# Delta-rule attention and a GELU layer on one core: another order of all engines' work

## The chip, the cores and the metric

The kernel runs on one core of one Trainium2 chip. The core has five engines that each work through a queue of their own: TensorE (PE in the profile; PEld is its weight load), VectorE (DVE), ScalarE (ACT), GpSimd (POOL) and SyncE (SP, which here issues DMAs only). ACT and POOL can issue DMAs too. The metric is the device time of one execution in microseconds (us), as the median of several runs; lower is better.

## The reference

Four batches of eight heads run a delta rule over 768 steps with a state of 48 x 48 per head; the outputs of all heads are put side by side, 3072 rows of 384, and go through two matrix products with a tanh GELU between them.

```python
k_n = k / (norm(k) + 1e-6)
for t in range(S):                       # S = 768, state is (4, 8, 48, 48)
    y[:, :, t] = q[:, :, t] @ state
    v_old = state @ k_n[:, :, t]
    state = state + beta[:, :, t] * outer(k_n[:, :, t], v[:, :, t] - v_old)
x = y.transpose(0, 2, 1, 3).reshape(3072, 384)
out = gelu_tanh(x @ w_in) @ w_out        # w_in 384 x 2048, w_out 2048 x 384
```

## The kernel before

The 768 steps are cut into 12 chunks of 64. A chunk is worked in two units of 16 heads, so 24 units, numbered 0 to 23; unit u belongs to chunk u // 2. Nothing in the kernel is a loop on the chip: every step is a word of its own, and each word is one or several instructions on one engine.

**A unit** (`prep`, L470 to L618). The words kc, kb and qb (L484 to L488) copy k, scaled k and q into bf16 with heads side by side. A transpose follows, on PE (T, Tk, Tc, Tb, Tq, L494, evicted by kT words) or by a DMA from SP (turn, L512). The words GM, GQ, G2 and G (L530) are products of keys with keys and queries, in quarters of the array; ln, wpm, wpq and wp (L534) write them under a triangular mask on DVE. Then the inverse of a 64 x 64 triangle for each head is made in five rounds. X10 and X11 (L564 on POOL, L566 on DVE) make the first guess. In round i, Ai (PE, eight products, L575), rti (DVE, 2I plus the product, L587) and Bi (PE, eight products) follow one another, and the result is copied from PSUM into the two diagonal blocks of `bd`. That copy has three forms, and the planner picked one for each round of each unit: two half copies bdei0 and bdei1 on ACT or DVE; one half bdfi0 and one whole with a scale, bdfi1 (L338); or one whole copy xii followed by two SBUF copies bdci0 and bdci1 on POOL or DVE (L617).

**A chunk** (`chain`, L620 to L714). K (L647) and Q are products of the state with keys and queries, vs (L657) scales v, R (L660) adds it to K's result, U (L670) multiplies by the inverse, Un copies that, S (L682) and Sn (L689) bring the state forward, O (L695) adds to Q's result, On copies it, and X on PE with xT, or a DMA turnx, transposes it for the layer. **The layer** (`mlp`, L716 on) has 16 up words per chunk (three matmuls each, L724), four gelu words (ACT, L728), eight down words (four matmuls each, L735: down0i and down1i for the two halves of the rows), two copies Z0 and Z1, and stores out.

**Around them.** The word norms sq, sum, pow, eps, nsq or nsa, inv and ib (L454 to L467) work out the norms of k; pow is ACT's square root in the first three chunks and POOL's power after these. The words k, q and v load one chunk's part, beta the betas, w1 and w2 (L441, L443) the weights in two halves each. tri, pad, bdz, ident, mup, mlo, two, half and the like set up constants. fill0 to fill69 (L394) are matmuls of zeros with zeros, of which a plan uses as many as it likes; nothing reads them.

**The order.** `ORDER` (L17 to L111) is a text of 1,708 words, found by a planner outside the kernel. A word is a step's name; a letter after a colon names its engine where the step may run on several (p, a, d, g, s for PE, ACT, DVE, POOL and SP; without it the first engine allowed is taken), a number after @ the PSUM bank where its result goes. `Flow.order` puts the words into one queue per engine in the order of the text, and `Flow.emit` works out the semaphore waits that the data need. Which copy, engine, bank and place in the queue a step gets is thus set by the text alone, and each engine runs its queue strictly in order.

```python
for i, word in enumerate(text.split()):
    word, _, bank = word.partition("@")
    name, _, e = word.partition(":")
    o = self.by[name]
    o.on, o.at = ENGINES[e] if e else o.engs[0], i
    ...
    self.queue.append(o)
    self.queues[o.on].append(o)
```

Of the kernel before, what the change touches and what calls it, by code (L numbers as in the profile page):

```python
# [16 lines left out]
ORDER = """  # L17
beta01:a one pad1 k0x1.11:a k0x0.01:a bdz0:g upone1 wz:d fill23@0 fill20@1 fill46@0 fill16@1 fill63@4 fill26@1 half:d fill25@0 fill12@2
fill54@5 ident pad3:g k0x0.10 tmplz:d tmpl0 k0x1.00:a k0x1.10:a k0x1.01:a mmup:d pad0 mmlo:d mlo0 fill64@0 k0x0.00 mlo1 tmpl1 two:d triln1:d
triwpm3:d triwpm1:d ladj16:d fill37@1 identf k0x0.11 ident2 ladj32:d fill28@4 sq.0a:d fill65@3 mup0 k1.00 fill56@4 sum.0a triln0:d fill41@1  # L20
fill52@6 beta00 betaT0@3 betaN000 betaN001 betaN010 betaN011 k1.01 epsb k1.10:a fill45@2 beta11:a k1.11 fill22@1 beta10 sq.0b:g tabS pow.0a
eps.0a twob:d J1.1@3 sum.0b q0.1 mup1 nsa.0a v0.11 inv.0a ib.0a upone0 v0.10 pow.0b fill55@2 q0.0:a eps.0b nsa.0b sq.1:d fill36@0 kb.0 kc.1
bdz1:g k2.10 fill49@2 inv.0b ib.0b:g kb.1:g betaT1@0 kc.0 Tc.1@1 fill9@2 betaA111 betaA110 betaA101 sum.1 pow.1 eps.1:g nsq.1:g kTc.1 q1.1
fill60@4 Tb.0@2 kTb.0 Tc.0@4 kTc.0 Tb.1@1 inv.1 triwpm0:d betaA100 ib.1 GM.0@6 ln.0 kb.3:g v1.11:a v0.01 X11.0 wpm.0 kTb.1:a GM.1@4 ln.1
X10.0 v0.00:a qb.0:a Tq.0@1 wpm.1 kc.3 Tk.3@2 triln3 A1.0@0 X10.1:d kTq.0 GQ.0@4 k2.00:a kTk.3:a q1.0:a X11.1 C1.1 rj1.1 rt1.0 B1.0@0 k2.01
pad2 kb.2 wpq.0 bde10.0 kc.2:d GM.3@6 ln.3 B1.1@1 bde10.1:d bde11.0 A2.0@0 rt2.0 bde11.1 A2.1@1 rt2.1 Tk.2@3 triwpm2 B2.0@2 B2.1@0 qb.1:a
v1.00 Tq.1@1 v1.10 v1.01 wpm.3 bde21.0:d k2.11 sq.2 sum.2 bde20.0 A3.0@2 fill1@4 fill4@5 fill42@4 fill14@5 q2.0 bdf20.1 bdf21.1:d A3.1@0
rt3.0 B3.0@2 kTk.2:a GM.2@4 rt3.1 triln2 ln.2 w2.1 qb.2:a bdz4:g bdz3:g X10.3 kTq.1:a X11.3 w1.1 A1.3@0 pad5:g pow.2 B3.1@1 k3.10 GQ.1@6
wpm.2 rt1.3 kc.5 k4.10 q2.1 bdf30.0 bdf31.0 A4.0@2 rt4.0 vs.1 B1.3@0 R0b.0:g bdf30.1 bdf31.1 A4.1@1 bdz2:g wpq.1 v2.00 bdf10.3 qb.3:g
eps.2:g B4.0@2 bde41.0 nsq.2:g bde40.0 X11.2 rt4.1 q3.0 X10.2 A1.2@4 rt1.2 B4.1@1 bde41.1:d w1.0 bde40.1 Tq.2@3 kTq.2 B1.2@4 bde10.2  # L30
triwpm4:g A5.0@5 rt5.0 A5.1@1 rt5.1 bde11.2 bdf11.3:d k3.01 B5.0@2 bde50.0 A2.2@3 rt2.2 B5.1@4 bde50.1:d bde51.0 k3.00 bde51.1 B2.2@0
bde21.2 bde20.2 inv.2 A2.3@1 rt2.3 R0a.0:g U.0@4 Un.0:d B2.3@1 A3.2@0 rt3.2 q4.0 Tq.3@2 O.0@4 On.0:d fill6@3 bde21.3 qb.5:g B3.2@0 bde20.3
A3.3@1 rt3.3 kTq.3:a GQ.3@6 X.0@2 xT.0:d B3.3@1 triwpm5:g bdf30.2 bdf31.2 A4.2@0 rt4.2 bdf30.3 bdf31.3:d up4.0@2 up12.0@4 up13.0 k3.11 wpq.3
ib.2:g kb.5:g B4.2@0 up5.0 up6.0 up7.0 up14.0 A4.3@1 up15.0 up0.0@6 q3.1 tabG bde41.2:d bde40.2 up1.0 up2.0 A5.2@0 rt4.3 gelu1.0 pad4:g
kb.4:g kc.7 up3.0 B4.3@1 w2.0 kc.4:g sq.3:g sum.3 k4.00 k5.10 q4.1 gelu3.0 gelu0.0 qb.4:g T.4@2 kT.4:a T.5@4 rt5.2 bde41.3:d bde40.3:d kT.5
pow.3 eps.3:g up8.0@6 up9.0 v2.11 A5.3@0 rt5.3 k5.00:a G2.5@2 ln.5 bdz5:g kc.6:g X11.5 k4.01:a G2.4@4 S.0@0 Sn.0 ln.4 X11.4 X10.4 G.4@2 wp.4
up10.0 qb.9:a up11.0 gelu2.0 nsq.3:g qb.6:g qb.7:g k4.11 K.1@0 R.1 inv.3 ib.3:g kb.6:g kb.7:g v3.11 G.5@4 wp.5 B5.2@2 sq.4 down10.0@3 A1.4@1
down00.0@0 bde51.2 rt1.4 kc.8 down01.0 X10.5 sum.4 pow.4 eps.4:g B5.3@4 bdf50.3 B1.4@1 bde10.4 k5.01 bde11.4:d down11.0 A1.5@5 rt1.5
down02.0 k5.11 sq.5:g kc.10:g A2.4@1 v4.10 v4.11 rt2.4 turn.7 v2.10 bdf51.3 bde50.2 B1.5@4 bde10.5:d bde11.5 down03.0 Z0.0 B2.4@2 v3.10
bde21.4:d kc.9:g U.1@6 Un.1 A2.5@5 rt2.5 q5.0 down12.0 GQ.2@0 wpq.2 Q.1@6 bde20.4 A3.4@2 turn.6 v3.00:a rt3.4 G2.7@4 O.1 On.1 S.1@0 Sn.1  # L40
nsq.4:g down13.0 inv.4 ib.4:g X.1@2 B2.5@6 xT.1:d kb.9:g v4.01 sum.5 pow.5 eps.5:g kb.8:g Z1.0 bde20.5 B3.4@7 bdf30.4 turn.9 fill47@3 v3.01
ln.7 bdf31.4 v2.01:a up0.1@0 up1.1 up2.1 up3.1 bde21.5:d gelu0.1 q6.1 A4.4@2 rt4.4 qb.8:a up8.1@4 up9.1 k7.00 A3.5@3 rt3.5 B4.4@2 bde41.4
k7.11 G2.6@0 ln.6 G.7@6 wp.7 q7.0 up10.1 B3.5@3 bde31.5 bde30.5 X10.6 up11.1 gelu2.1 up4.1@0 up5.1 up6.1 G.6@6 bde40.4:d A4.5@3 k6.10:a
# [755 lines left out]
```

## Time and profile before

| | |
|---|---|
| median of 3 runs | 263.77 us (263.1 to 265.27) |
| span of the profiled execution, first to last instruction | 258.8 us |
| DVE busy in the span | 209.5 us, 358 instructions |
| ACT busy | 185.1 us, 295 instructions |
| POOL busy | 136.2 us, 198 instructions |
| bytes read and written in HBM | 20.64 and 4.72 MB |

The profile is of one execution. The times of the three runs have more around them than the span: the median is 5.0 us above it. A row such as "L587 DVE TENSOR_TENSOR rt<-ps,two 128x512 bf16<-128x512 f32 x71 | 47.6, 683 | 5.4 <-PE ps L575 4.9" reads: line, engine, operation, what is written from what, shapes, number of instructions, us busy in all, mean ns of one, us that the engine was idle just before them, and what ended most of that. The windows give for each stretch the us that each engine was busy and, in brackets, its instructions; then the TensorE clock that was granted as a share of full speed, the busy share of the DMA engines, and the rate of the DMAs.

### The profile page before, as it was taken

To read this page: it belongs to the slowest core of one execution; us is meant where nothing else is said; L and a number is where in the kernel's file an instruction comes from. 1 tells how busy PE (TensorE), PEld (TensorE's weight loads), DVE (VectorE), ACT (ScalarE), POOL (GpSimd) and SP (SyncE) were. 2 spreads that over 40 slices of the span, in tenths; PEclk is the share of its full clock that TensorE was granted. 3 is DMA by queue.
4 is the path that set the end of the run, shared out by engine and by line. 5 is a ranking of instruction groups with operands and counts; after the bars stand their busy time and mean duration, and the time that the engine had idled before them with its cause. 6 is when DMAs were issued, how large, how long until landed. Compare 5 with 4: busy or idle time off the path is not lost.

```text
span 258.8 us, 12244 instructions
## 1 busy us (share of the span) xinstructions
PE 242.1 (94%) x5490; PEld 189.6 (73%) x5490; DVE 209.5 (81%) x358; ACT 185.1 (72%) x295; POOL 136.2 (53%) x198
## 2 busy tenths in 40 slices
PE   7769789998999999999999999989989999999994
PEld 2446669666867878778877787768868878877672
DVE  6898998988999798899999788997778879895000
ACT  0679899667786878687978879866948745754452
POOL 4469767997558978688158255643654204130000
PEclk9985999999999999999999999999999999999999
DMA  5999999879999877959729959536935720004122
GB/s 88 200 191 182 212 185 200 135 132 151 164 198 146 167 107 134 159 102 165 160 47 157 155 96 185 53 74 123 155 66 106 128 48 4 3 5 124 30 63 61
DMA packets 116788, 31.46 MB, mean 122 GB/s; under 512 B 110848, under 2 KB 115968, under 8 KB 116736
## 3 DMA queue, kind: packets, MB, share of 16 engines
q1 hardware_dynamic: 98096, 24.24, 57.4%
q0 software_dynamic: 2880, 3.15, 7.5%
q10 hardware_dynamic: 15760, 3.30, 7.4%
q8 instruction: 43, 0.70, 1.1%
q14 instruction: 9, 0.07, 0.1%
HBM read 20.64 MB, written 4.72 MB: 98 GB/s over the span
## 4 chain that ended last, share of the span: by engine, by line
PE 81%; DVE 8%; POOL 4%; issue 3%; ACTq 2%; ACT 1%; POOLq 0%
PE ps L724 24%; PE ps L735 24%; PE ps L575 20%; PE ps L530 4%; PE ps L647 3%; PE ps L670 2%; PE ps L695 2%; ACTq L432 2%; DVE rt L587 1%; PE ps L682 1%; DVE wp L534 1%; POOL nrm L458 1%; DVE ln L534 1%; PE ps L394 1%; POOL bd L564 1%
## 5 line engine op out<-in xcount | busy, mean ns | idle before, releaser
L332 ACT ACTIVATE bd<-ps 64x512 bf16<-64x512 f32 x127 | 72.8, 587 | 20.5 <-PE ps L575 18.7
L724 PE MATMUL ps<-xT,W 128*128 128x256 bf16 x576 | 76.3, 273 | 0.7 <-issue 0.7
L735 PE MATMUL ps<-W,gT 128*128 128x384 bf16 x384 | 73.8, 326 | 0.0
L728 ACT ACTIVATE gT<-ps 128x1024 bf16<-128x1024 f32 x48 | 48.5, 1020 | 15.1 <-PE ps L724 14.7
L724 PEld LDWEIGHTS ps<-xT,W 128*128 128x128 bf16 x576 | 50.7, 98 | 7.2 <-issue 1.0
L587 DVE TENSOR_TENSOR rt<-ps,two 128x512 bf16<-128x512 f32 x71 | 47.6, 683 | 5.4 <-PE ps L575 4.9
L735 PEld LDWEIGHTS ps<-W,gT 128*128 128x128 bf16 x384 | 33.0, 97 | 16.9 <-ACT gT L728 0.2
L564 POOL TENSOR_SCALAR_AFFINE_SELECT bd<-ln 64x512 bf16<-64x512 bf16 x44 | 29.1, 664 | 24.5 <-DVE ln L534 20.9
L332 DVE CAST bd<-ps 64x512 bf16<-64x512 f32 x51 | 34.8, 686 | 5.2 <-PE ps L575 4.2
L534 DVE CAST_PREDICATED wp<-mup,ps 128x1024 bf16<-128x1024 uint16 (+1 forms) x28 | 29.7, 1062 | 1.5 <-PE ps L530 1.4
L575 PE MATMUL ps<-rt,bd 128*128 128x64 bf16 x576 | 28.5, 195 | 2.0 <-DVE rt L587 1.5
L458 POOL TENSOR_TENSOR nrm<-nrm,half 128x16 f32<-128x16 f32 x9 | 26.2, 2908 | 7.6 <-DVE nrm L456 7.4
L617 POOL COPY bd<-xi 64x256 f32<-64x256 f32 x27 | 10.8, 404 | 34.6 <-DVE xi L332 19.5
L575 PE MATMUL ps<-wp,bd 128*128 128x64 bf16 (+1 forms) x576 | 27.1, 189 | 1.5 <-POOL bd L564 1.0
L575 PEld LDWEIGHTS ps<-rt,bd 128*128 128x128 bf16 x576 | 23.5, 99 | 6.7 <-DVE rt L587 2.4
L575 PEld LDWEIGHTS ps<-wp,bd 128*128 128x128 bf16 x576 | 23.0, 98 | 6.2 <-POOL bd L564 1.5
L587 DVE TENSOR_TENSOR rl<-ps,two 128x384 bf16<-128x384 f32 (+1 forms) x48 | 23.0, 484 | 4.8 <-PE ps L575 4.4
L575 PE MATMUL ps<-ln,bd 128*128 128x48 bf16 (+1 forms) x384 | 18.8, 190 | 2.8 <-issue 1.6
L575 PE MATMUL ps<-rl,bd 128*128 128x64 bf16 x384 | 18.8, 193 | 0.7 <-DVE rl L587 0.7
L575 PEld LDWEIGHTS ps<-ln,bd 128*128 128x128 bf16 x384 | 15.5, 98 | 5.2 <-issue 1.8
L575 PEld LDWEIGHTS ps<-rl,bd 128*128 128x128 bf16 x384 | 15.7, 98 | 3.0 <-DVE rl L587 1.1
L485 POOL TENSOR_TENSOR tok<-kraw,nrm 128x384 bf16<-128x384 f32 x19 | 15.6, 829 | 4.2 <-PE ps L682 2.7
(98 smaller groups left out, 327.3 us busy)
## 6 DMA issues: line engine op xcount, KB each, us to landing
qraw<-in_q_dram SPq DMA_DIRECT2D x21, 192.0 KB, 5.0
out_dram<-ob SPq DMA_DIRECT2D x21, 192.0 KB, 3.4
vraw<-in_v_dram SPq DMA_DIRECT2D x38, 96.0 KB, 3.3
...
W<-in_moe_w_in_dram POOLq DMA_DIRECT2D x2, 768.0 KB, 10.1
...
```

The source lines that it names most:

```text
L332: return e.activation(out, in_, ACT.Copy) if e is nc.scalar else e.tensor_copy(out, in_)
L458: if e is nc.scalar else e.tensor_tensor(nr[:, 1, hx], nr[:, 0, hx], half[:, hx], ALU.pow), reads=[nrn, "half"] + ["one", "roots"] * (c < ...
L485: A(("dve", "pool"), op("kb"), lambda e, P: e.tensor_tensor(kb, kr, nr[:, 5, hx].unsqueeze(2).to_broadcast(full), ALU.mult), reads=[f"kraw ...
L530: ins = e.matmul(o, kT[s][r, y, g, hf(a)], src)
L534: return e.copy_predicated(out.rearrange("p (x g) t -> p x g t", x=2), mask[:, 0:wd].bitcast(U16).unsqueeze(1).unsqueeze(1).to_broadcast([ ...
L564: A(("pool", "dve"), op(f"X1{a}"), lambda e, P, src=ln[m][hf(a), :, :], dst=bd[b_][hf(a), :, hf(a)], a=a: e.affine_select(out=dst, in_=src ...
L575: ins = e.matmul(P(name)[:, C * h + cs.start:C * h + cs.stop], bd[b_][:, h, :], rhs[:, h, cs], **kw)
L587: A(("dve",), op(f"rt{i}"), lambda e, P, i=i, cs=cs, cn=cn, r_=r_: e.tensor_tensor(r_[:, :, cs], P(ps(f"A{i}")).rearrange("p (h t) -> p h ...
L617: A(("pool", "dve"), op(f"bdc{i}{a}"), lambda e, P, src=xi[i_][hf(a), :, :], dst=bd[b_][hf(a), :, hf(a)]: e.tensor_copy(dst.bitcast(F32), ...
L724: ins = e.matmul(P(ph)[:, 256 * f:256 * f + 256].rearrange("p (x t) -> p x t", x=2), W1[:, j, 128 * (i + f):128 * (i + f) + 128], x_[:, :, ...
L728: A(("act",), f"gelu{i // 4}.{c}", lambda e, P, i=i, ph=ph: e.activation(g_[:, i:i + 4, :], P(ph).rearrange("p (f t) -> p f t", f=4), ACT. ...
L735: ins = e.matmul(P(po)[:, 0:DM], g_[:, f, 128 * b:128 * b + 128], W2[:, f, :], start=(f == 0), stop=(f == FC - 1))
```

## The change

Only the text `ORDER` is replaced. The set of words is the same, with the same 31 fills and for every step the same choice among its forms (18 turn and 7 turnx, for example, and the same form of copy into `bd` in each round); the order, the engines and the PSUM banks are others. The planner that found it counted the fetch of TensorE's instruction blocks as well; how it did so isn't part of the kernel.

Words by engine, where the two texts differ most:

| kind | before | after |
|---|---|---|
| bde (half copies into `bd`) | 101 ACT, 47 DVE | 115 ACT, 33 DVE |
| X10, X11 | 44 POOL, 4 DVE | 38 POOL, 10 DVE |
| bdc | 27 POOL, 5 DVE | 21 POOL, 11 DVE |
| qb | 12 ACT, 12 POOL | 4 ACT, 5 DVE, 15 POOL |
| kc | 9 ACT, 2 DVE, 13 POOL | 6 ACT, 5 DVE, 13 POOL |
| loads of k, q, v | 28 ACT, 96 SP | 48 ACT, 76 SP |
| stores | 3 ACT, 23 SP | 8 ACT, 18 SP |

PE has 684 words in both, DVE 358, and without DMAs ACT has 293 before and 297 after, POOL 190 and 186.

The diff, cut to the beginning, to the words around X.0 and down00.0, and to the end:

```diff
-ORDER = """
-beta01:a one pad1 k0x1.11:a k0x0.01:a bdz0:g upone1 wz:d fill23@0 fill20@1 fill46@0 fill16@1 fill63@4 fill26@1 half:d fill25@0 fill12@2
-fill54@5 ident pad3:g k0x0.10 tmplz:d tmpl0 k0x1.00:a k0x1.10:a k0x1.01:a mmup:d pad0 mmlo:d mlo0 fill64@0 k0x0.00 mlo1 tmpl1 two:d triln1:d
...
-eps.0a twob:d J1.1@3 sum.0b q0.1 mup1 nsa.0a v0.11 inv.0a ib.0a upone0 v0.10 pow.0b fill55@2 q0.0:a eps.0b nsa.0b sq.1:d fill36@0 kb.0 kc.1
-bdz1:g k2.10 fill49@2 inv.0b ib.0b:g kb.1:g betaT1@0 kc.0 Tc.1@1 fill9@2 betaA111 betaA110 betaA101 sum.1 pow.1 eps.1:g nsq.1:g kTc.1 q1.1
...
-bde21.2 bde20.2 inv.2 A2.3@1 rt2.3 R0a.0:g U.0@4 Un.0:d B2.3@1 A3.2@0 rt3.2 q4.0 Tq.3@2 O.0@4 On.0:d fill6@3 bde21.3 qb.5:g B3.2@0 bde20.3
-A3.3@1 rt3.3 kTq.3:a GQ.3@6 X.0@2 xT.0:d B3.3@1 triwpm5:g bdf30.2 bdf31.2 A4.2@0 rt4.2 bdf30.3 bdf31.3:d up4.0@2 up12.0@4 up13.0 k3.11 wpq.3
...
-out00.10 out11.10 up5.11 up8.11@4 up2.11 up3.11 up9.11 up13.11 up14.11 up15.11 up6.11 up10.11 up7.11 up11.11 gelu0.11 down00.11@6
-down10.11@7 gelu1.11 gelu2.11 down01.11 down11.11 down12.11 gelu3.11 down13.11 down02.11 down03.11 Z1.11 out10.11:a Z0.11 out11.11
-out00.11:a out01.11
-"""
+ORDER = """pad4:g bdz5:g ident:g wz:g mmlo:g tmplz:g tmpl0 tmpl1 k0x1.10:a k0x1.11:a k1.00:s triwpm4:d k0x1.00:a bdz2:d pad0:d k0x0.11:a fill9@0 k0x1.01:s epsb:g
+triln1:d pad1:d k0x0.01:a k1.01:a k0x0.00:s k0x0.10:s beta01:a identf fill60@1 k1.10:a bdz3:g two:a triwpm1:d triln0:d one:g ladj32:d twob:a k1.11:s beta00:s
+mmup:g beta10:s mup0 mup1 fill4@2 triwpm0:d fill22@0 tabS beta11:s triln3:g bdz0:g triln2:g ladj16:d kc.1:g half:g ident2 mlo0 sq.0b:d sum.0b sq.0a:a v0.11:s
+k2.01:s Tc.1@0 betaT0@1 kc.0:d sum.0a triwpm5:g kTc.1:d Tc.0@2 pow.0b fill46@3 q0.0:a pow.0a eps.0a:d pad2:g betaN000 upone1 eps.0b:g nsa.0b nsa.0a sq.1:a
...
+bde21.2:a B2.3@3 ln.4 w2.1 X10.4:g A3.2@2 Un.0:a G.4@4 Tq.2@6 O.0@0 q4.1:s rt3.2 X11.4:g bde21.3:a qb.7:g X11.5:g B3.2@2 bde20.3:a fill28@7 On.0:a vs.1:g
+sq.3:g kTq.2:d k5.00:a A3.3@3 bdf30.2:a G.5@6 X.0@0 wp.4 rt3.3 tabG S.0@4 bdf31.2:a kc.6:g xT.0:d Sn.0:a B3.3@3 A4.2@2 up12.0@0 k5.01:a rt4.2 bdf30.3:a up13.0
...
+up8.0@0 bde11.4:a up9.0 nsq.4:d kc.8:a rt5.3 B5.3@6 pow.3 eps.3:g bde10.4:a B1.5@2 up10.0 up11.0 A2.4@7 kc.7:d nsq.3:g down00.0@3 inv.3 sq.5:g gelu1.0 v2.10:a
...
+gelu2.11 gelu3.11 down01.11 down03.10 Z0.10:a Z1.10:d out11.10:s down02.11 down03.11 down10.11@1 down11.11 out00.10:s down12.11 down13.11 Z0.11:d out00.11:a
+Z1.11:a out01.11:s out11.11:s out10.11:a"""
```

More of the change, by code (lines that the diff above doesn't have):

```diff
@@ L25 @@
[L25 to L28, printed above, removed]
@@ L37 @@
[L37 to L40, printed above, removed]
@@ new lines @@
+kc.20:d bde20.16:a bde21.16:a up7.6 down11.5 bdc30.15:g A3.16@0 B2.17@2 G2.19@4 gelu1.6 bdc31.15:g G2.18@6 A4.15@3 vs.8:g rt3.16 bde21.17:a rt4.15 out11.3:a
+v9.10:s ln.18 bde20.17:a down12.5 down00.5@0 B3.16@2 v10.00:a bde31.16:a A3.17@3 B4.15@6 ln.19 down13.5 up12.6@4 v9.00:a rt3.17 sq.11:g bde40.15:d up13.6
+bde30.16:d up14.6 ib.10:g qb.22:g qb.20:d up15.6 sum.11 pow.11 B3.17@7 down01.5 bde41.15:a bde31.17:a A4.16@6 bde30.17:a down02.5 rt4.16 gelu3.6 X11.18:g
+A4.17@7 A5.15@2 rt4.17 down03.5 G.18@4 Z0.5:a Z1.5:d G.19@6 X11.19:g rt5.15 out00.4:s B4.17@1 down00.6@0 wp.18 B4.16@2 bde41.17:a wp.19 qb.21:a bde40.17:d
```

151 lines of the change are left out of this document (75 added, 76 removed).

## The prediction

> **What bounds the kernel now.** I read the page first, then the chain of waits in order of time, the grouped lines by form, the table of windows, and last PE's own timeline.
>
> ```profile
> span 258.8 us, 12244 instructions
> ...
> PE 242.1 (94%) x5490; PEld 189.6 (73%) x5490; DVE 209.5 (81%) x358; ACT 185.1 (72%) x295; POOL 136.2 (53%) x198
> ...
> PE   7769789998999999999999999989989999999994
> ...
> DVE  6898998988999798899999788997778879895000
> ...
> PEclk9985999999999999999999999999999999999999
> ...
> q8 instruction: 43, 0.70, 1.1%
> ...
> PE 81%; DVE 8%; POOL 4%; issue 3%; ACTq 2%; ACT 1%; POOLq 0%
> ```
>
> TensorE (PE) is the bound for most of the span, and the chain that ended last runs 81% through it. VectorE (DVE) holds 8% of the chain, and its row of tenths is full just where PE's has gaps, in the first ten slices (65 us). The same in windows:
>
> ```profile
> core 0: us, PE busy (x) PEld busy (x) DVE busy (x) ACT busy (x) POOL busy (x), PEclk, DMA share, GB/s
> 0.00:49.48 49.48, 40.21 (x843) 29.41 (x844) 44.46 (x101) 36.15 (x66) 33.04 (x60) 0.93 1.15 179
> 0.00:74.68 74.68, 64.30 (x1415) 47.70 (x1416) 67.20 (x134) 55.48 (x96) 52.29 (x85) 0.95 1.11 169
> ...
> 84.30:146.00 61.70, 61.16 (x1534) 49.95 (x1533) 55.02 (x89) 50.89 (x81) 42.73 (x58) 1.00 0.82 137
> 206.00:255.05 49.05, 49.02 (x915) 37.75 (x914) 27.18 (x44) 26.38 (x37) 6.27 (x10) 1.00 0.16 37
> ```
>
> Up to 49.48 us DVE is busy for 44.46 and PE for 40.21. From 84 us on PE is busy for 61.16 of 61.70 and 49.02 of 49.05. PE's busy time flatters it, since matmuls overlap. What a word of the order costs when nothing holds PE up is read from the dense pieces of the chain:
>
> ```profile
> 63.84 0.47 PE ps L530 x32
> 68.48 0.70 PE ps L575 x24
> 72.83 0.63 PE ps L647 x64
> 74.68 0.54 PE ps L670 x16
> ...
> 244.94 5.24 PE ps L724 x48
> 250.18 5.21 PE ps L735 x32
> ```
>
> A product of eight (A, B words) is 0.70/3 = 0.23 us, a G or GQ word 0.24, a K or Q word 0.32, an up word 5.24/16 = 0.33, a down word 5.21/8 = 0.65. So two things can be gained: the head, where PE waits for DVE, and holes inside the PE-bound rest.
>
> **The change part by part.** Both orders hold the same 1,708 words, 684 of them PE's, 31 of these fills. PE's own work is unchanged; only when it runs can change. I counted words in the two lists and priced each by the mean duration of its group (engine, line and shape); the rows of the kinds that weigh most:
>
> ```profile
> L332 DVE CAST bd<-ps 64x512 bf16<-64x512 f32 x51 | 34.8, 686 | 5.2 <-PE ps L575 4.2
> L332 DVE CAST us<-ps 128x768 bf16<-128x768 f32 x2 | 1.9, 954 | 0.7 <-PE ps L670 0.7
> L332 DVE CAST xi<-ps 128x512 bf16<-128x512 f32 x5 | 3.4, 685 | 0.2 <-PE ps L575 0.2
> L534 DVE CAST_PREDICATED wp<-mup,ps 128x1024 bf16<-128x1024 uint16 x20 | 24.3, 1213 | 1.4 <-PE ps L530 1.4
> L443 POOL DMA_DIRECT2D W<-in_moe_w_out_dram x2 | 2.1, 1030 | 2.0 <-DMA vraw<-in_v_dram 2.0
> L441 POOL DMA_DIRECT2D W<-in_moe_w_in_dram x2 | 1.6, 805 | 0.0
> ```
>
> *The head.* Take word U.2 (L670, started at 74.68 above; a word is one step, its letter the kind and its number the unit or chunk). Ahead of it the old list has 135 DVE words and the new one 121. Nine bde copies go to ACT (9 x 0.686 = 6.2 us), so do On, Un (2 x 0.954, the rows of us and xo agree) and two xi (1.4); with a bdf copy (0.7), set-up words moved to POOL and ACT and a few small ones, 13.9 us leave. One wp more (1.2), one ln, sum, kb, kT, R0b, two X1, two bdc and small ones bring 7.6 back: 6.3 us less by mean durations. Neighbours on DVE overlap (67.20 busy for words that sum to 75.4, or 0.89), so 5.6 us less. But PE has also done less by then: four down, one up, one A2 and one Q fewer, two G more, 2.6 + 0.3 + 0.2 + 0.3 - 0.5 = 3.0 us. Net 2.6 us. The same count at down00.0 (49.48) gives 15 DVE words fewer, 5.1 us x 44.46/51.5 = 4.4, with 0.8 us more PE work ahead: 5.2 net. I take 3.2, nearer the later point, since the rest follows from that one. The ends are 0 (POOL takes over, below) and 5.2.
>
> ACT takes the copies: 9 more bde ahead of U.2 on an engine that was busy 55.48 of 74.68. Its idle 19 us hide them. Over the whole span the words of DVE fall by some 3.3 us, those of POOL by 2.6, ACT's rise by 1.6; past 84 us that lies beside PE and counts nothing.
>
> *DMA issues.* 24 more loads and stores are issued from ACT (33 become 57) and as many fewer from SP.
>
> ```profile
> 8.54 0.62 ACTq L423 DMA_DIRECT2D qraw<-in_q_dram  x1
> ```
>
> This issue starts 0.01 us after an ACT word that runs until 8.74, so it runs beside it. Bounds: 0, and 24 x 0.62 = 15 us of ACT's 73.7 idle us. I take 0. If the cover is gone (a load that must wait for its buffer), what is queued behind it are the bd copies and gelus, and PE waits for them.
>
> *Instruction blocks.* PE's idle time that nothing but its own issue ended:
>
> ```profile
> PE ps L575 <- issue: 1.9, 3, 0.9
> ...
> PE ps L724 <- issue: 0.7, 1, 0.7
> ...
> PE ps L695 <- issue: 0.4, 1, 0.4
> ...
> PE ps L530 <- issue: 0.3, 1, 0.3
> PE ps L682 <- issue: 0.3, 1, 0.3
> ...
> 60.18 0.72 PE L724 MATMUL ps<-xT,W 128*128 128x256 bf16 x5
> 61.58 0.28 PE L724 MATMUL ps<-xT,W 128*128 128x256 bf16 x1 [0.68 <-issue]
> ...
> 0.00:46.20 46.20, 37.11 (x728) 27.11 (x728) 41.28 (x96) 33.91 (x62) 30.05 (x54) 0.93 1.16 180
> 0.00:61.30 61.30, 51.20 (x1107) 36.85 (x1107) 55.26 (x116) 45.30 (x81) 43.00 (x74) 0.94 1.08 166
> 0.00:77.00 77.00, 66.44 (x1489) 49.23 (x1489) 69.52 (x138) 57.13 (x99) 53.08 (x87) 0.96 1.11 170
> ```
>
> Seven holes, 3.6 us. Each cuts a word in two, as the fifth and sixth matmul of an up here; counted from the start of the last matmul before it, each costs about 0.2 more, so 5.0 us in all. The windows end inside the first three: 1,456, 2,214 and 2,978 loads and matmuls had run, 758 and 764 apart. With the waits among them that is 768 = 3 x 256 each time, and 0.70 MB in 43 packets is 16 KB a packet: blocks of 256 instructions, and PE stands still at a border where the next one has not come. The Trainium skill, "Runtime: NRT & Kernel Launch", section "Instruction fetch mechanics", has blocks of that size and calls the crossing "mostly hidden". The trace agrees on the size; seven borders of 43 were not hidden. By the page alone this term would be 0, and the sum below 260.9.
>
> A border is late where 256 instructions pass quickly, which is where K, Q, S, O words stand together. Cut into such blocks and priced as above, the old list has six blocks under 3.5 us past the head, shortest 1.7 and 2.5. The new one has eight (Q.5 G.15 O.5 S.5, and Q.10 S.10 O.10 stand nearly side by side), shortest 2.5 and 2.9. So the worst are relieved and more middling ones made. Bounds: all 5.0 gained, or 2 lost. I take a gain of 0.6.
>
> *The start.* Before, 24 PE words, 17 of them fills, precede the first transpose Tc.1; after, four fills.
>
> ```profile
> 1.72 4.96 PE L394 MATMUL ps<-wz 128*128 128x512 bf16 x16 [1.72 <-DVE half L359]
> 18.10:24.90 6.80, 5.81 (x64) 4.33 (x65) 6.26 (x10) 6.42 (x12) 6.19 (x9) 0.50 1.32 181
> ```
>
> The clock was full after these sixteen and fell to half once, for 6.8 us. Without them the half clock probably lasts from the start into the first products. Bounds: 0, and one such window on PE's path, 3.4 us. Before, DVE still set the pace around that window, so I take a loss of 0.3.
>
> *Sum.* 258.8 - 3.2 - 0.6 + 0.3 = 255.3 us of span. The three runs have a median of 263.77, 5.0 above the span. Forecast 260.3.
>
> **The rivals.**
>
> *The head and the blocks both come out in full.* 258.8 - 5.2 - 5.0 + 5.0 = 253.6. For it: DVE's row of tenths is full there. Against: the quick blocks that remain.
>
> *POOL takes DVE's place, no change.* Ahead of X.0 (36.9 us before) POOL's words rise from 35 to 63, 18.7 to 35.0 us by mean durations, and all four W issues (3.7 us) stand there too, against three: 38.7 us of work from 0.8 on. If POOL sets the pace, X.0 comes at 39.5, 2.6 later with 1.9 more PE work done: a loss of 0.7 where I have a gain of 3.2. 258.8 + 0.7 - 0.6 + 0.3 + 5.0 = 264.2. Against it: the presets among these words and sq.3, vs.1 are not needed for X.0.
>
> *The clock stays at half through the head, slower.* From Tc.1 to U.0 the new list has 14 us of PE work at full clock and 23 fills of 0.22. If two windows of 6.8 us pass at half clock with PE on the path, 6.8 us are added: 258.8 - 3.2 - 0.6 + 6.8 + 5.0 = 266.8. It decides from about one window and a half (5.1 us) on. For it: the fills left out. Against: 5.81 busy of 6.80 in the half window, after which the clock came back. The Trainium skill, "TensorE: Matmul & The Clock Gate", section on the clock gate, has about 3.4 us of sustained work lift the half rate; by that one window at most is lost and this rival falls.
>
> **How the numbers follow.** Chances: forecast 0.45, in full 0.12, POOL 0.22, half clock 0.21. A measurement of this kernel can tell about 1% (2.6 us) from no change. The forecast's own range, 256.5 to 262.5, has a fifth above 261.1. Faster by over 1%: 0.12 + 0.36 = 0.48; within 1%: 0.09 + 0.18 = 0.27; slower: 0.21 + 0.04 = 0.25. The range goes from 254.0 to 267.0, into both outer cases.
>
> **What would show it.** Right: U.2 about 71 to 72 us in the trace with bd copies on ACT ahead of it; fewer than seven cut words, or as many but shorter; PE's share of the chain above 81% and DVE's below 8%. Wrong: POOL in the chain before X.0 with more than 4%; more than one 5 among the first digits of PEclk; cut words that cost more than 5 us; ACT waiting with a load at the head of its queue.

## The result: 7% slower, and the profile after

| | before | after |
|---|---|---|
| median of 4 runs each, same chip | 263.44 us (261.92 to 265.27) | 283.21 us (279.61 to 285.47) |
| ratio, 95% interval | | 1.0707 (1.0619 to 1.0795) |
| span of the profiled execution | 258.8 us | 281.5 us |

Forecast were 260.3 us and a range of 254.0 to 267.0. The page of the changed kernel:

```profile
span 281.5 us, 12204 instructions
...
PE 248.9 (88%) x5480; PEld 191.4 (68%) x5490; DVE 217.3 (77%) x358; ACT 189.7 (67%) x300; POOL 135.9 (48%) x194
...
PE   2798867789977988996999999999997999999994
...
PEclk9999979999999799999799999999999999999999
...
PE 56%; DVE 17%; ACT 9%; issue 6%; DMA 5%; POOL 3%; ACTq 2%; SPq 1%; POOLq 0%
```

No engine's busy time grew by more than 8 us, yet PE holds 56% of the chain that ended last where it held 81%. DVE's share doubled from 8%, ACT's went from 1 to 9%, and DMA, absent before, has 5%: no new bound, but many new waits of PE. PE's row has gaps up to the nineteenth slice (134 us), and from there on it is as full as before but for one slice at 211 to 218 us. Lines of the program stand 7 lower than before in this trace, and one to six lower in the experiments' traces.

To compare two orders, I read each at the same amount of PE work: the start of a PE word, less the work of the PE words ahead of it at the prediction's dense prices (fills left out, 211.8 us in all). What is left is the time lost up to there:

| PE work done | before | after | after, run again | x2 (below) |
|---|---|---|---|---|
| 5 us | 13.4 | 18.5 | 17.6 | 16.2 |
| 45 us | 28.0 | 37.2 | 34.4 | 35.7 |
| 65 us | 31.0 | 47.4 | 43.0 | 40.9 |
| 90 us | 33.6 | 54.4 | 48.4 | 44.9 |
| 150 us | 39.6 | 60.6 | 54.7 | 51.2 |
| 211 us | 43.3 | 65.8 | 59.6 | 54.1 |

Against the kernel before, the change loses 4 to 5 us at the start, 2 to 4 more up to 45 us of PE work, 6 to 7 between 45 and 65 (82 to 112 us of its trace), 3 to 4 up to 90, and little after that.

### The profile page after: what moved, and what is told of

Same layout as the page of the kernel before. It is cut to its first block, busy times and chain, and to the rows that moved or that the text cites. A ratio compares the mean times of both kernels' runs of the same rounds, so it can differ in the third digit from the quotient of the medians.

```text
span 281.5 us, 12204 instructions
## 1 busy us (share of the span) xinstructions
PE 248.9 (88%) x5480; PEld 191.4 (68%) x5490; DVE 217.3 (77%) x358; ACT 189.7 (67%) x300; POOL 135.9 (48%) x194
## 4 chain that ended last, share of the span: by engine, by line
PE 56%; DVE 17%; ACT 9%; issue 6%; DMA 5%; POOL 3%; ACTq 2%; SPq 1%; POOLq 0%
PE ps L717 18%; PE ps L728 15%; PE ps L568 14%; DMA kT<-tok 5%; ACT bd L325 5%; PE ps L523 3%; DVE rt L580 3%; DVE wp L527 2%; ACTq L425 2%; PE ps L663 2%; DVE bd L325 1%; DVE ln L527 1%; ACT gT L721 1%; DVE tok L325 1%; PE ps L640 1%
## 5 line engine op out<-in xcount | busy, mean ns | idle before, releaser
L325 ACT ACTIVATE bd<-ps 64x512 bf16<-64x512 f32 x135 | 78.6, 589 | 37.2 <-PE ps L568 34.0
L717 PE MATMUL ps<-xT,W 128*128 128x256 bf16 x576 | 79.0, 274 | 0.5 <-DVE rl L580 0.3
L728 PE MATMUL ps<-W,gT 128*128 128x384 bf16 x384 | 76.5, 331 | 0.1
L721 ACT ACTIVATE gT<-ps 128x1024 bf16<-128x1024 f32 x48 | 48.4, 1019 | 15.9 <-PE ps L717 15.6
L557 POOL TENSOR_SCALAR_AFFINE_SELECT bd<-ln 64x512 bf16<-64x512 bf16 x38 | 25.5, 676 | 37.5 <-DVE ln L527 34.5
L325 DVE CAST bd<-ps 64x512 bf16<-64x512 f32 x43 | 29.1, 682 | 3.3 <-PE ps L568 2.6
L580 DVE TENSOR_TENSOR rl<-ps,two 128x384 bf16<-128x384 f32 (+1 forms) x48 | 23.2, 485 | 11.0 <-PE ps L568 10.6
L527 DVE CAST_PREDICATED wp<-mup,ps 128x1024 bf16<-128x1024 uint16 (+1 forms) x28 | 29.6, 1063 | 0.4 <-PE ps L523 0.2
L610 POOL COPY bd<-xi 64x256 f32<-64x256 f32 x21 | 8.6, 412 | 39.8 <-ACT xi L325 20.1
L523 PE MATMUL ps<-kT 48*64 48x64 bf16 (+1 forms) x832 | 17.5, 211 | 6.4 <-DMA kT<-tok 2.4
L527 DVE CAST_PREDICATED ln<-mlo,ps 128x512 bf16<-128x512 uint16 x24 | 16.3, 686 | 6.2 <-PE ps L523 4.5
L478 POOL TENSOR_TENSOR tok<-kraw,nrm 128x384 bf16<-128x384 f32 x19 | 16.4, 869 | 7.1 <-PE ps L675 6.1
```

Of the source, the lines that this page charges most:

```text
L325: return e.activation(out, in_, ACT.Copy) if e is nc.scalar else e.tensor_copy(out, in_)
L478: A(("dve", "pool"), op("kb"), lambda e, P: e.tensor_tensor(kb, kr, nr[:, 5, hx].unsqueeze(2).to_broadcast(full), ALU.mult), reads=[f"kraw ...
L523: ins = e.matmul(o, kT[s][r, y, g, hf(a)], src)
L527: return e.copy_predicated(out.rearrange("p (x g) t -> p x g t", x=2), mask[:, 0:wd].bitcast(U16).unsqueeze(1).unsqueeze(1).to_broadcast([ ...
L557: A(("pool", "dve"), op(f"X1{a}"), lambda e, P, src=ln[m][hf(a), :, :], dst=bd[b_][hf(a), :, hf(a)], a=a: e.affine_select(out=dst, in_=src ...
L580: A(("dve",), op(f"rt{i}"), lambda e, P, i=i, cs=cs, cn=cn, r_=r_: e.tensor_tensor(r_[:, :, cs], P(ps(f"A{i}")).rearrange("p (h t) -> p h ...
```

## The experiments

Line numbers of kernels aside, every edit is to the text `ORDER` alone. Four theories were set against each other: a cold TensorE clock at the start; late loads behind ScalarE's words; VectorE's copies held up beside POOL; and an order so tightly chained that a wait taken away is replaced by the next one. Measured beside each of them, the kernel before took 262.6 to 263.4 us.

**The same kernel again.** It is told first, because it sets what a difference is worth.

> The changed kernel once more, unchanged. Five of the edits to it (table load, casts, loads on SP, fills at the start, fills in the holes) measured 277.1 to 277.8 us, each 5 to 6 us below its 283.21 us, though the holes that each edit closes are worth 1 to 4 us in its trace. If 283 us is what the kernel takes: 282 to 284.5 us again. If the kernel itself varies from one run to the next by where the half-clock windows and the long fetches fall: 279 to 281 us, and each of the five edits is worth half of what its ratio said or less.

278.9 us (276.99 to 282.37, 6 runs), ratio 1.0624 (1.0567 to 1.0682). Both times together the change costs some 17 us, ten runs from 277.0 to 285.5. What varies is seen in the traces: in the first profile the clock fell to half three times behind the start, in the second never. Over the ten runs the time goes with the mean clock that was granted: 277.0 us at 0.994 and 1.000, 278.6 to 279.6 at 0.988, 280.8 to 285.5 at 0.976 to 0.982.

```profile
core 0: us, PE busy (x) PEld busy (x) DVE busy (x) ACT busy (x) POOL busy (x), PEclk, DMA share, GB/s
89.80:92.00 2.20, 0.26 (x9) 0.13 (x5) 0.68 (x1) 1.18 (x2) 2.04 (x2) 1.00 1.43 128
93.10:96.40 3.30, 3.30 (x54) 2.39 (x56) 2.13 (x5) 1.93 (x4) 1.98 (x3) 0.50 1.46 160
```

In these windows of the first trace PE does nearly nothing for 2.2 us, and 1.0 us later the granted clock is 0.50 for 3.4 us. In the repeat the hole at the same place is 1.4 us. So single edits that measure 5 us below 283.2 are worth less: I go by what each does to its own hole, and by runs of the same mean clock, where the unchanged kernel's 277.0 us at 0.994 and 1.000 is the measure.

**The start.** e1_warm puts eleven fills ahead of the first four:

```diff
-k0x0.11:a fill9@0
+k0x0.11:a fill0@0 fill2@1 fill3@2 fill5@3 fill7@0 fill8@1 fill10@2 fill11@3 fill13@0 fill15@1 fill17@2 fill9@0
```

> The changed order with eleven more fills ahead of its first four, nothing else. Theory A (the clock is at half until 21.4 us because four fills are not enough, and PE's first words run late for it): the granted clock is full before 10 us, the first matmuls of eight (line 568) take 0.41 instead of 0.64 us, GM.0 and A1.0 come 2 to 4 us earlier, and the time falls by 3 to 5 us from 283.2. Theory D (the head waits for data and for VectorE, the half clock only fills waiting time): the clock is full but the time falls by less than 1.5 us.

277.06 us, 1.0553 (1.0463 to 1.0643). But the lost time at 5 us of PE work is 18.8, where it was 18.5, and the first words came no sooner. The clock was full from 6.3 us only up to 13.2 and at half again up to 20.0, so this run leaves open what a full clock through the start would give. The eleven fills alone, at least, gain nothing there. ScalarE's timeline of the changed kernel shows what the first words wait for:

```profile
6.23 1.28 ACT L363 ACT_TABLE_LOAD   x1 [6.23 <-issue]
7.52 0.26 ACT L363 ACTIVATE two<-tmpl 128x64 f32<-128x64 bf16 x1
7.68 0.24 ACT L363 ACTIVATE twob<-tmpl 128x64 bf16<-128x64 bf16 x1
7.94 1.28 ACT L349 ACT_TABLE_LOAD   x1
9.23 0.20 ACT L349 ACTIVATE one<-one 128x1 f32<-128x1 f32 x1
9.34 0.51 ACT L447 ACTIVATE sq<-kraw 128x384 f32<-128x384 f32 x1
```

Two function-table loads of 1.28 us follow each other. The new order runs the copies two and twob ahead of tabS, the square root; the first load is for the copies and the second for the square root. Before, tabS was ScalarE's first word (the copies were DVE's), and one load served all. The Trainium skill, "ScalarE: Activation LUTs", section "Table sets: the hidden batching unit", has cheap functions such as copy in every set, so the order of the first words decides how many loads there are; by that page a switch costs about 2.7 us with its drain, and the trace has 1.28 and no pause beside it. e9_table_once turns the order round:

```diff
-pad4:g bdz5:g
+one:d pad4:g bdz5:g
...
-bdz3:g two:a triwpm1:d triln0:d one:g ladj32:d
+bdz3:g tabS two:a triwpm1:d triln0:d ladj32:d
...
-fill22@0 tabS beta11:s
+fill22@0 beta11:s
```

> The changed kernel with two words of ScalarE's start moved: the memset one goes to the head of VectorE's queue and tabS (the square root that loads ScalarE's function table) ahead of two and twob; in the changed kernel the copies two and twob run first, and the trace shows a table load of 1.28 us before them and a second one of 1.28 us at 7.94 us before tabS, both in the chain of waits; the kernel before has one at its start. If the second load is a cost on the path: one load at the start, sq.0a begins near 8.1 us instead of 9.34, and the time falls by 1.0 to 1.3 us, to 281.9 to 282.2 us, with the gain there already when TensorE has done 5 us of work. If the start is bound by another chain (POOL's ident2 at 7.6 us, the clock): the same 283.2 us within 0.5, with Tc.1 and Tb.0 where they were.

277.6 us, 1.0502 (1.0382 to 1.0623); one load is left. Lost time at 1 us of PE work is 13.2 for 14.1, at 14 us of work 24.7 for 26.7. So the second load is a cost on the path. Against the repeat, though, nothing is left of the gain at 5 us of work, and by 14 us the repeat is ahead. The expected 1.0 to 1.3 us is borne out by 0.9 here and 1.4 in x2, below. The rest of the 5.6 lies elsewhere in its trace or in the spread of the unchanged kernel.

**ScalarE's DMA queue.** e3_one_load moves one load, e4_loads_on_sp 43 loads and stores from ScalarE to SP in place; e8_before_loads_after gives the loads and stores of the kernel before the changed kernel's queues (39 from SP to ScalarE, 15 the other way).

```diff
-kb.11:g k7.01:a bde31.6:a
+kb.11:g k7.01:s bde31.6:a
```

> The changed order with one letter changed: the load k7.01 is issued from SyncE instead of ScalarE. Theory B (the load stands behind the copy On.2 on ScalarE and is issued 8 us after its three sisters; sq.7 on GpSimd waits 4.7 us for it, X10.9 is queued behind sq.7 and TensorE waits 2.2 us for that): k7.01 is issued before 80 us, the 2.2 us hole at A1.9 closes, the time falls by 1.5 to 2.5 us. Theory D: GpSimd's wait goes, but the time stays within 1 us, since the next wait is as late.

> The changed kernel's order with 43 of the loads and stores that it issues from ScalarE (the loads of chunk 3 and later, and the stores but those of the last half chunk) issued from SP instead, in the same places of the order. If ScalarE's queue is what makes loads late (the load k7.01 issued 10 us behind its sisters, VectorE's and POOL's words waiting for it): at least 3 us faster than the changed kernel, 280 us or less, and the hole ahead of A1.9 gone. If a load only changes the queue in which it stands behind others (SP also issues the transposes kT and xT, which wait for copies): within 2 us of 283 us or slower, with the holes at U.1, K.1 or G2.23 longer, since transposes land later.

> The kernel before with its 54 DMA-issuing words whose queue the change moves (39 from SP to ScalarE, 15 the other way) on the changed kernel's queues, nothing else. The prediction costed this at nothing: then 263 to 264.5 us. If a load that must wait on ScalarE's queue holds up the copies behind it, or is late behind them, wherever it stands: 266 us or more, with ScalarE's idle time ended by DMA in the trace.

e3: 281.35 us, 1.069 (1.0573 to 1.0807). e4: 277.84 us, 1.0558 (1.0462 to 1.0653). e8: 277.17 us, 1.0509 (1.0404 to 1.0615), 14 us slower than the kernel whose order it has. In the changed kernel's trace, first ScalarE's timeline, then POOL's:

```profile
84.69 0.81 ACT L325 ACTIVATE xo<-ps 128x768 bf16<-128x768 f32 x1 [1.82 <-PE ps L688]
84.69 0.60 ACTq L425 DMA_DIRECT2D kraw<-in_k_dram  x1
```

```profile
89.96 1.47 POOL L448 TENSOR_TENSOR sq<-kraw 128x768 f32<-128x768 f32 x1 [4.73 <-DMA kraw<-in_k_dram]
91.38 0.66 POOL L557 TENSOR_SCALAR_AFFINE_SELECT bd<-ln 64x512 bf16<-64x512 bf16 x1
```

The load k7.01 stands behind On.2 (xo) in ScalarE's queue. On.2 waits for PE's O.2, which a block border holds up until 84.2, so the load is issued at 84.7; its sisters went out from 74 to 76 us. POOL has sq.7 at the head of its queue and waits 4.73 us, X10.9 stands behind it, and PE's A1.9 has a hole of 2.2 us. With the load on SP, in e3, sq.7 runs at 84.60 without a wait, and the hole ahead of A1.9 is 2.2 us all the same. POOL's and DVE's timelines of e3 show why:

```profile
87.39 2.90 POOL L656 TENSOR_TENSOR vraw<-vraw,nrm 128x768 f32<-128x768 f32 x2
```

```profile
87.70 2.93 DVE L565 TENSOR_TENSOR bd<-ln,twob 64x512 bf16<-64x512 bf16 x1
```

X11.9 on DVE took 2.93 us, where the changed kernel has 0.42 for it. POOL, no longer waiting, ran vs.3 and vs.4 at that time, and X11.9 was over just behind them. This is the fourth theory at work, with a mechanism.

In e8 the largest part is one place. ScalarE and SP issue two loads of v, one of q, two transposes, three of k and a store between 121.2 and 129.2 us. Its chain of waits, DVE's timeline, and windows over that place:

```profile
123.75 6.85 DMA vraw<-in_v_dram
...
130.67 1.47 POOL vraw L651
132.15 2.87 POOL nrm L452
```

```profile
132.18 0.96 DVE L654 TENSOR_TENSOR rs<-ps,vraw 128x768 bf16<-128x768 f32 x1 [6.97 <-POOL vraw L651]
```

```profile
123.60:131.00 7.40, 3.91 (x100) 3.29 (x96) 1.61 (x3) 5.15 (x9) 0.33 (x1) 1.00 1.22 168
131.80:141.90 10.10, 7.45 (x72) 5.57 (x73) 6.12 (x12) 2.10 (x3) 4.21 (x5) 0.50 0.02 4
```

The loads of v take 6.85 us to land, and POOL's vs waits 8.67 us for them. DVE's R.5 (rs) adds vs to K's result and waits 6.97 us. PE's up8.4 needs the PSUM banks that R.5 frees and starts 0.05 us after R.5's end, so PE has a hole of 5.7 us, and behind it the clock is 0.50 for 10 us. The next block of PE's instructions also landed only as the burst ended, at 131.60 us, so the fetch may have held PE nearly as long; the wait that ended last is R.5. The lost time grows by 12.6 us between 80 and 100 us of PE work, and by 1.9 in the kernel before. Whether the queue alone, in the changed order, costs anything is less plain: in e4's trace the hole ahead of A1.9 shrinks to 0.6 us, but the time gains nothing at the same clock (279.1 us at 0.994, 276.1 at 1.000).

**VectorE beside POOL.** One of the three longest holes behind the start, and in the repeat the longest, stands ahead of B3.10. DVE's timeline of the changed kernel, then POOL's:

```profile
129.76 2.60 DVE L325 CAST tok<-qraw 128x384 bf16<-128x384 f32 x1
132.28 0.55 DVE L478 TENSOR_TENSOR tok<-kraw,nrm 128x384 bf16<-128x384 f32 x1
132.86 1.29 DVE L580 TENSOR_TENSOR rt<-ps,two 128x512 bf16<-128x512 f32 x2
```

```profile
129.72 0.82 POOL L478 TENSOR_TENSOR tok<-kraw,nrm 128x384 bf16<-128x384 f32 x1
130.50 0.21 POOL L455 TENSOR_TENSOR nrm<-nrm 128x16 f32<-128x16 f32 x1
130.68 1.47 POOL L650 TENSOR_TENSOR vraw<-vraw,nrm 128x768 f32<-128x768 f32 x1
```

qb.17 began 0.04 us after a run of three POOL words and was over 0.2 us after the run. By form, such casts take 0.35 us before (two of them) and 0.79 to 0.82 after (ten). The Trainium skill, "SBUF — State Buffer", section "Who interferes with whom", has DVE's copies and casts in SBUF, and its operations with two SBUF inputs, compete with POOL for one pair of ports, the copies and casts where they run in a mode with two ports; the loser is blocked for the whole instruction. The trace agrees, and more: the loser waited here for three instructions in a row. e2_casts_on_act puts the nine qb and kc of units 7 and later that stood on DVE on ScalarE:

```diff
-bde21.11:d qb.17:d eps.9:g
+bde21.11:d qb.17:a eps.9:g
```

> The changed order with its nine late kc and qb copies of VectorE put on ScalarE in the same places of the order. Theory C (VectorE's copies in SBUF are held up while GpSimd works: qb.17 took 2.60 us, kc.7 1.26, kc.20 1.45, where 0.35 is usual): the hole of 2.2 us between K.5 and B3.10 closes, and the time falls by 2 to 4 us. Theory D (ScalarE is as late as VectorE, the hole is filled by another wait): less than 1 us.

277.49 us, 1.0587 (1.0513 to 1.066), and at a mean clock of 0.992 to 0.994 (276.5 to 278.4 us) about the unchanged kernel's time. The hole ahead of B3.10 stays at 1.9 us, since kb.15 moved up into qb.17's place beside the same POOL words:

```profile
125.70 2.80 DVE L484 TENSOR_TENSOR tok<-kraw,nrm 128x384 bf16<-128x384 f32 x1
```

x1_no_dve_copies takes both away:

```diff
-bde21.11:d qb.17:d eps.9:g
+bde21.11:d eps.9:g
...
-out00.1:a kb.15:d rt3.10
+out00.1:a rt3.10
...
-vs.5:g bdf31.11:a
+vs.5:g qb.17:g kb.15:g bdf31.11:a
```

> The changed kernel with two words moved from VectorE to POOL, behind vs.5: the casts qb.17 (2.60 us in its trace, where the same cast takes 0.36 us elsewhere) and kb.15. In e2_casts_on_act, where only qb.17 left VectorE, kb.15 came into the same place and took 2.80 us, ending 0.4 us behind POOL's run of kb, nsq and vs. If a VectorE word that reads only SBUF is held until POOL's run is over: VectorE goes straight on to rt3.10, the hole ahead of B3.10 falls from 2.2 us to 0.6 us or less, the half clock of 3.4 us right behind it goes too, and the time falls by 3 to 4 us against the unchanged kernel of this call. If rt3.10 is late for another reason (ScalarE, the matmul A3.10): the hole stays above 1.5 us, and the time within 1 us.

275.31 us, 1.0493 (1.0435 to 1.055), 3.6 below the unchanged kernel measured beside it; at a mean clock of 0.994 to 1.000 it is 1.6 to 2.8 (274.2 to 275.4 us). DVE goes from bde21.11 to rt3.10:

```profile
125.12 0.69 DVE L331 CAST bd<-ps 64x512 bf16<-64x512 f32 x1
126.35 1.29 DVE L586 TENSOR_TENSOR rt<-ps,two 128x512 bf16<-128x512 f32 x2 [0.53 <-PE ps L574]
```

The hole (2.7 us in the repeat) is gone. Between 80 and 110 us of PE work 1.6 us less are lost than in the repeat: this is what the place is worth, and the half clock that followed it in the first trace costs some 1.7 more when it comes (an estimate: half of its 3.4 us).

**Fills in the holes.** e10_filled puts 29 fills into four holes.

```diff
-B3.7@0 A1.9@6
+B3.7@0 fill10@2 fill11@3 fill13@7 fill15@6 fill17@2 fill18@3 fill19@7 fill21@6 A1.9@6
```

> The changed kernel with 29 more fills in four of its holes behind the start (8 ahead of A1.9, 7 ahead of B3.10, 6 ahead of A4.2, 8 ahead of G2.23; at 0.22 us each they are shorter than the holes of 2.2, 2.2, 1.5 and 2.3 us). In the trace of the changed kernel the clock drops to half for 3.4 us right behind the holes at 89.6 and 131.1 us. If the drop follows from TensorE's pause: no half clock at these two places, and 2 to 3.5 us less, 279.7 to 281.2 us. If the clock goes its own way: half clock there or elsewhere as before, and 283 us within 1.

277.48 us, 1.054 (1.0469 to 1.0611): the half clock is gone at both places. But it was gone in the repeat too, behind holes of 2.2 us (at O.2, 7 us ahead of A1.9) and 2.7 us (B3.10) without fills, and at the same mean clock the time is about the unchanged kernel's. A pause of 2 us can bring the half clock; whether it does varies with the run. That fills prevent it is not shown.

c2_before_warm does the like for the kernel before, with eighteen fills in ten gaps of its head:

```diff
-bde11.0 A2.0@0
+bde11.0 fill15@0 fill17@0 fill18@0 A2.0@0
```

> The kernel before with eighteen more fills, put into ten gaps that TensorE has between 8.5 and 24.7 us (0.4 to 0.9 us each; the fill ahead of the word that waits). The profile of before has the clock at half from 18.1 to 24.9 us. If the half clock there follows from the gaps and costs about half of its 6.8 us: 260 to 262 us, and no half clock between 16 and 37 us. If the words that feed TensorE set the time there and not its clock, or if the fills come in the way of the words: 263.5 us or more.

267.75 us, 1.0159 (1.0076 to 1.0243), slower. 1.6 us more are lost up to 5 us of PE work, and the 36 instructions move every block border behind them. PE's weight loads and a window show the worst one:

```profile
66.40 0.64 PEld L569 LDWEIGHTS ps<-rt,bd 128*128 128x128 bf16 x11 [2.85 <-issue]
```

```profile
65.60:72.20 6.60, 5.80 (x51) 4.33 (x51) 1.25 (x2) 3.08 (x5) 3.40 (x3) 0.50 0.84 159
```

A border, where PE goes from one block of 256 instructions to the next, held PE for 2.85 us, and half clock followed for 6.8 us. This trace is of a run of 270.9 us. The other three, 266.8 to 268.7 us, had a mean clock of 0.999 to 1.000, so no half clock, and are slower than the kernel before all the same, whose trace has 6.8 us of it. A full clock in the head, bought with these fills, gained nothing.

**Engines or order.** e6_after_engines_before gives 202 words of the new order their old engines, e7_before_engines_after gives the same words of the old order the new ones; h1_before_then_after has the old order up to U.5 and the new one behind it. The beginning of e7's edit:

```diff
-beta01:a one pad1 k0x1.11:a
+beta01:a one:g pad1:d k0x1.11:a
...
-tmpl1 two:d triln1:d triwpm3:d
+tmpl1 two:a triln1:d triwpm3:g
```

> The changed kernel's order with the 202 words that are no DMA and had moved between VectorE, ScalarE and POOL put back on the engine they had before. If the choice of engine is the cause (POOL's longer words, casts on VectorE beside POOL, bd copies on ScalarE): most of the 20 us goes, to 272 us or below. If it is the order, and the plan is chained so tightly that any word that is late passes its lateness on: no better than 278 us, and it may be slower than 283 us, since the order was laid out for the other engines.

> The mirror image: the order of the kernel before with those 202 words on the engines that the changed kernel gives them (DMA-issuing words stay). If the engines are the cause: 272 us or more. If the order is: below 268 us. If both matter only together (each order laid out for its engines), both this run and its mirror image are slower than the kernel whose order they use.

> The order before up to the word U.5, then the remaining words in the changed order. U.5 started at 127.4 us before and at about 148 after. If the loss arises ahead of U.5 (start, late loads, held copies, fetch stalls in the head): within 2.5 us of the time before, 263 to 267. If the changed order loses as much per chunk throughout: 270 to 275.

e6 and e7: 297.12 us (1.1271, 1.1168 to 1.1374) and 326.22 us (1.237, 1.2266 to 1.2474): each order is laid out for its engines, and neither half of the change can be called the cause. h1 takes 273.04 us, 1.0419 (1.0337 to 1.0501). That is the time expected of an order that loses throughout, but for another reason: most of it is lost at the seam, where PE has a hole of 7.5 us and then a clock of 0.50 for 10.2 us. From K.7 (120 us of PE work) on, it needs 97.7 us to the last down word; the kernel before needs 97.4 for as much work, the changed one 99.0. The new order's second half costs 0.3 us in h1 and 1.6 in the changed kernel.

**Repairs together.** c1_three_undone joins e9, e2, e3 and e1; c3_all adds e4's move to SP, the two words of x1 and twelve fills in two holes.

> The changed kernel with four repairs in one: tabS ahead of the two copies (one function-table load at the start), nine casts from VectorE to ScalarE, k7.01 issued from SP, and eleven more fills ahead of the first four. Alone they measured 1.0502, 1.0587, 1.069 and 1.0553 of the kernel before, where the unchanged one measured 1.0707. If the causes are separate and add: 0.02 + 0.012 + 0.002 + 0.015 less, 1.02 of before, about 269 us. If the next wait fills each gap (a chained plan): no better than the best one alone, 1.045 or more, about 275 us or more.

> All repairs in one: one table load, the casts off VectorE (qb.17 and kb.15 to POOL, the other eight to ScalarE), 43 loads and stores from ScalarE to SP, eleven more fills at the start, and six fills each ahead of A4.2 and G2.23. If the causes are separate and their local gains in the traces add (2 to 3.4 us at the start, 2.5 at the late loads, 2 with 1.7 for the clock at B3.10, 1 at G2.23, 1.5 of half clock elsewhere), 10 to 11 us below the unchanged kernel's trace of 281.5 us: 270 to 273 us. If they add as their ratios said: 262 us or less. If the next wait takes each one's place: 275 us, no better than c1_three_undone.

c1: 275.1 us, 1.0379 (1.0269 to 1.0489). c3: 280.34 us, 1.0599 (1.0514 to 1.0684), no better than the unchanged kernel. In c1 the start is nearly repaired: 15.1 us lost at 5 us of PE work, 18.5 in the first trace of the change, 13.4 before. Then other holes take it back. PE's weight loads, c1 first, then c3, whose trace is of a run of 284.6 us:

```profile
53.32 0.72 PEld L723 LDWEIGHTS ps<-xT,W 128*128 128x128 bf16 x5 [3.60 <-issue]
```

```profile
37.16 0.30 PEld L530 LDWEIGHTS ps<-kT 48*64 48x64 bf16 x16 [3.94 <-DVE rl L587]
...
57.90 0.19 PEld L575 LDWEIGHTS ps<-rt,bd 128*128 128x128 bf16 x3 [3.27 <-issue]
```

The rows that end in "issue" stand at block borders. The other one, 3.94 us ahead of G2.5, is a wait for a load. The chain of waits ahead of it:

```profile
23.79 10.46 DMA kraw<-in_k_dram
...
34.32 1.48 POOL sq L455
...
35.82 0.95 DVE nrm L456
36.77 0.34 DVE rl L587
```

G2.5 needs a PSUM bank that DVE's rt5.1 (rl) frees. rt5.1 stands behind sum.4 (nrm) in DVE's queue, sum.4 waits for POOL's sq.4, and sq.4 for a load of k that took 10.46 us to land; PE starts 0.05 us after rt5.1. The load itself is on SP in the changed kernel too; what made it late here is not shown. Both edits also change the number of PE's instructions, and with it the words that stand at the borders.

So x2_named_holes leaves PE's stream alone and moves eight words of other engines: e9's two, x1's two, and

```diff
-down12.1 sq.7:g
+down12.1 X11.9:g X10.9:g sq.7:g
...
-v5.00:s kb.12:g
+v5.00:s X11.11:g kb.12:g
...
-rt4.18 v10.10:s
+rt4.18 turn.23 v10.10:s
```

(X11.9, X10.9, X11.11 and turn.23 taken out where they stood.)

> The changed kernel, TensorE's stream untouched, with eight words of other engines moved so that five named holes close: tabS ahead of two and twob (start), qb.17 and kb.15 to POOL (ahead of B3.10), X11.9 to POOL and it and X10.9 ahead of sq.7, which waits for a late load (ahead of A1.9), X11.11 to POOL ahead of kb.12 (ahead of B3.9), and the transpose turn.23 ahead of two loads on SP (ahead of G2.23). In the trace of after_again these holes are worth about 1.0, 1.7, 1.4, 1.3 and 1.4 us. If they are causes that add: 272 to 274 us, where after_again took 278.9 us, with the five holes at 0.7 us or less. If the next wait takes their place, as in c3_all: 277 us or more. The time of the kernel before, 263 us, is out of reach in either case, since the rest of the start, the fetches of instruction blocks and the shorter waits stay.

271.57 us (270.54 to 275.43, 6 runs), 1.034 (1.027 to 1.0409), 0.4 us below what was expected if the causes add; the four holes behind the start are under 0.7 us each, and 1.4 us less are lost at 5 us of PE work.

```profile
span 269.7 us, 12217 instructions
...
PE 246.4 (91%) x5490; PEld 188.7 (70%) x5490; DVE 212.2 (79%) x355; ACT 188.3 (70%) x299; POOL 138.9 (51%) x197
...
PE 63%; DVE 15%; ACT 11%; DMA 4%; issue 3%; POOL 2%; ACTq 0%; SPq 0%; POOLq 0%
```

Eight of 1,708 words are worth 7.3 us against the repeat. At a mean clock of 0.994 alone they are worth some 5.5 (270.5 to 271.7 us where the unchanged kernel took 277.0), which is also what the two traces differ by; the rest is half clock. The next wait did take something back: the border at A5.3 holds PE for 2.9 us, where it was 1.7 in the repeat. No version here beats the kernel before.

## Why the prediction was wrong, step by step

**What bounds the kernel: right, and misread.** PE is the bound before, with other engines just in time. A step that is just in time has no price of its own, and I took that from PE's fullness to mean that a reordering could only gain where PE waits. The costs came where the old order had no wait.

**The head, -3.2: failed.** It was to be seen at U.2 at 71 to 72 us. U.2 starts at 80.36 us (77.61 in the repeat), before at 74.68, and with 3.1 us less of PE's work ahead of it: 8.8 us more lost there, 6.1 in the repeat. I had counted right (14 DVE words fewer), and the count was the wrong measure: it adds busy time up over 75 us, and PE waits for single words in a chain. At the start the word is not even DVE's but ScalarE's table load. And the step "its idle 19 us hide them", of the copies that go to ACT, is the one that failed. Ahead of X.0, the chain of waits has DVE for 20.2 us before and 12.6 after (14.5 in the repeat), as was wanted, but ACT for 2.2 before and 10.6 after (14.0 in the repeat), and X.0 comes 8.2 us later (5.5 in the repeat), with under 2 us more of PE's work ahead of it. Pieces of that chain in order of time, the kernel before first:

```profile
32.95 0.59 DVE bd L332
...
34.88 0.59 ACT bd L332
...
35.50 0.59 ACT bd L332
```

```profile
30.53 0.59 ACT bd L325
31.12 0.57 ACT bd L331
...
34.04 0.59 ACT bd L325
...
34.66 0.60 ACT bd L325
```

In the changed kernel eight copies into `bd` follow each other on ACT from 30.5 to 35.3 us, all of them in the chain; in the repeat the chain runs on ACT alone from 29.6 to 38.5. Idle time elsewhere in the head did not help a queue that was full just here. What these copies cost by themselves is not shown: no run moved them alone, and e6, which gives them back with all the others, is slower still.

**The start, +0.3: mis-sized, and its cause named too narrowly.** At 5 us of PE work 5.1 us more are lost than before (4.2 in the repeat). About 1 of that is the second table load (0.9 in e9, 1.4 in x2). The clock was at half until about 21 us in the first trace, seen in PE's rows rather than in PEclk, which has no entry before:

```profile
19.50 0.63 PE L387 MATMUL ps<-wz 128*128 128x512 bf16 x1
...
20.35 0.64 PE L568 MATMUL ps<-wp,bd 128*128 128x64 bf16 x8
21.51 0.40 PE L568 MATMUL ps<-wp,bd 128*128 128x64 bf16 x8
```

Eight products of one kind take 0.64 us and, 1.2 us later, 0.40. Of the bounds 0 to 3.4 the start broke the upper one; the rival with a clock at half through the head came near in length, but not in price: e1 lifted the clock up to 13.2 us and gained nothing at the start, while c1, which removed the table load as well and had a full clock from 5.8 us on, gained 3.4 (2.5 against the repeat). That is more than the table load, so the clock probably was on the path behind it; no run has a full clock with both loads, so its own price is not shown. 1.7 us of the start stay unexplained.

**The blocks, -0.6: wrong in sign, small.** The seven stalls of before add up to 4.4 us, the three of the changed kernel to 5.3 and the five of its repeat to 5.6 (gaps between weight loads, 0.1 us taken off each): a loss of about 1. Two of the three, from PE's weight loads:

```profile
56.19 0.15 PEld L568 LDWEIGHTS ps<-wp,bd 128*128 128x128 bf16 x3 [1.76 <-issue]
...
84.24 0.29 PEld L688 LDWEIGHTS ps<-us,wp 64*64 64x64 bf16 x25 [1.84 <-issue]
```

The mechanism was right. What I left out is that the fetch itself is late where the DMA engines are full. In eight traces, the fetch starts a median 0.9 us after PE crossed the last border where the DMA engines were under 30% busy in between (112 borders), and 1.9 us where they were full (154 borders), with 4 to 5.7 us common around 40 to 55 us. It lands about 1 us later, and PE goes on 1.2 to 1.9 us after the landing. The length of a block, which I had counted, is only one side of it.

**DMA issues, 0: failed.** My ground was that an issue runs beside a word of ScalarE. It does; the cost is another. A load in ScalarE's queue goes out when the word ahead of it does, and that word may wait for PE. The prediction had named the reverse case, words waiting behind a load. e8 gives 14 us for the whole move in the old order, most of it behind one burst; in the new order it is the hole at A1.9, 2.2 us or 1.4 in the repeat, of which e3 alone recovered nothing.

**Moves between engines, at nothing past 84 us: failed.** Casts and X11 words went to DVE where POOL works beside them: 2.60 us for 0.36 at qb.17, 1.38 for 0.42 at X11.11. x2's words there took the time back. I priced each by its mean, which holds only where POOL is quiet.

**The rivals.** POOL taking DVE's place gave 264.2, and its mark was over 4% of the chain before X.0: POOL is not in that stretch of the chain at all, and has 3% of the whole. In that stretch ACT took DVE's place. Slower was right as a side, at a chance of 0.25, and 283 lay beyond every case, since no case let small waits add up. Of the repeat's 16.3 us, 5.5 net are recovered by x2's eight words, about 1 is the blocks; the rest, some 10 us, 2.8 of it at the start, is spread over short waits, ACT's copies in the head perhaps among them, that these runs did not separate.
